# One exponential for four token tiles of A's keys, V's weights loaded early, and a new order

## The chip, the cores and the metric

The kernel runs on one core of a Trainium2 chip. A core has five engines with queues of their own: TensorE (PE) multiplies matrices, ScalarE (ACT) computes the exponentials, VectorE (DVE) evicts and combines, GpSimd (POOL) adds, SyncE (SP) issues transfers (ACT issues a few as well). PE's weight loads are listed as PEld. The time is the device time in microseconds (us), the median of several runs; lower is better.

## The reference

Two attention blocks on 2048 tokens of width 512, with 32 heads of 16 each, lie side by side in the output. A is linear attention: each key and query goes through phi, and the keys' products with V are summed over all tokens. B is full softmax attention.

```python
qkv = (x @ wqkv).reshape(B, S, 3, H, Dh).transpose(2, 0, 3, 1, 4)      # H = 32, Dh = 16, S = 2048
# A
phi = lambda t: jnp.where(t > 0, t + 1, jnp.exp(t)) + 1e-6
pq, pk = phi(q), phi(k)
kv = jnp.einsum("bhsd,bhse->bhde", pk, v)
z = jnp.einsum("bhsd->bhd", pk)
o = jnp.einsum("bhqd,bhde->bhqe", pq, kv) / (jnp.einsum("bhqd,bhd->bhq", pq, z)[..., None] + 1e-6)
# B
p = softmax(jnp.einsum("bhqd,bhkd->bhqk", q, k) * Dh ** -0.5)
o = jnp.einsum("bhqk,bhkd->bhqd", p, v)
# both: o.transpose(0, 2, 1, 3).reshape(B, S, D) @ wo;  out = concatenate([a, b], axis=-1)
```

## The kernel before

**B's scores.** They are cut into 2048 blocks of 128 keys by 512 queries for one head. Four heads share PE at a time, in groups g of 32 rows; a unit u is four heads (one of each row group) and one of four chunks of 512 queries, 64 blocks. `NU` is 32 units. Each block is computed by one matmul (`qk`, L872) and goes one of two ways.

- The first way is ACT's. Three blocks, then two (`ABL`), lie in one of two PSUM buffers `SCR` (pS in the profile); one ACT instruction (L1049) takes their exponential into `PT`, a ring of 3 rows with 2 slots each. One product with V (`pv_cand`, L1130) then adds a block into the PSUM tile pPV.
- The second way approximates the exponential in integers. DVE scales a block out of one of two PSUM banks `DBANK` (pD) into int16 (`d_emit`, L957), and those bits, read as float16, are the first of three terms. POOL adds two shifts to two such blocks at a time (`shifts`, L981) for the other two terms. Each term has V scaled by its own factor, so a block costs PE three products, not one.

A unit's sum ends with a transpose, a reciprocal and a multiplication (`unit_done`, L1185 to L1197).

**Jobs.** Everything else comes in jobs with stages on several engines, which use the banks of pD: projections of B's Q, K (`proj_job`, L595) and V (`v4_job`, L678; evicted by L683, and scaled twice by L687), a bound on B's scores (`gram_job`, `flag_job`), A's work, and the output projections (`omm_job`, L788). For A, `akv_job` takes two token tiles of 128 and one of four groups bq of 128 columns: 16 matmuls (L709), two evictions by DVE into `KNa` and `VNa`, then `phi_stages`: ACT's exponential into `EA` (L698), and on DVE max(t, 0) + 1e-6 (L700) and min(exp, 1) + that (L701). `akvsum_job` multiplies the 16 tiles of KNa and VNa into the state. The next bq's keys wait for it. A's queries go through `phi_stages` as well, 512 columns at a time. DVE's instructions with the key `PORT` and POOL's additions are ordered by semaphores so that they don't run at the same time.

**The order.** It is planned when the kernel is built, not on the chip. The planner keeps a clock for each engine (T), candidates with costs and due times, and picks the next instruction one by one; what it appends is what each engine runs, in that order, with semaphores between them. The numbers by which it chooses (`NAMES`) come from the table `POLICY`, one row for each 8 us of its own PE clock, 86 rows; `SEED` is that of a small random term. Costs such as 0.051 + n * 0.000833 us for an exponential over n columns stand in the code. Jobs wait in lists: `urgent`, `early` (the first projections of B, ten of them), `bjobs`, `urgent2`, `ajobs`. `d_pick` decides whether a block may go the second way now. `filler` puts matmuls that change nothing (zeros into pPV, L1348, or the identity into a free bank, L1357) into gaps of PE's plan that are long enough; `pe_opt` wraps each candidate of PE and adds `PH` where PE changes its kind of work.

**The loads.** SP issues B's x and weights in a fixed order, ACT two of them; V's columns of B's weights come as one load after the first transposing load of x.

**The end.** The last four token tiles' output projections are prepared by `pre_job`; `last_job` adds the last matmul (L815), an eviction (by ACT, ACT, DVE, ACT) and the store (L820), issued by SP after DVE's eviction and by ACT after its own.

Of the kernel before, what the change touches and what calls it, by code (L numbers as in the profile page):

```python
# [232 lines left out]
def bass_concat_heads__linear_attn_block__softmax_full_mha__prompt_kernel(nc, A_x, A_wqkv, A_wo, B_x, B_wqkv, B_wo, out):  # L233
# [14 lines left out]
    UB = NT * 4  # L248
    DEND = 12
# [4 lines left out]
    POLICY = [  # L254
        (0.15, 3.5, 4.2, 0, 3, 4, 32, 3.0, 1.0, 16, 10.0, 0.0, 0, 0, 0, 1, 0.0, 0.0, 2.0),
        (0.25, 3.5, 4.2, 0, 3, 4, 20, 3.0, 1.0, 16, 10.0, 0.0, 0, 0, 0, 1, 0.0, 0.0, 1.0),
        (0.25, 3.5, 3, 0, 3, 4, 20, 3.0, 0.5, 16, 10.0, 0.0, 0, 0, 0, 1, 0.0, 0.0, 1.0),
        (0.15, 3.5, 4.2, 0, 3, 4, 32, 3.0, 1.0, 16, 10.0, 0.0, 0, 0, 19, 1, 0.1, 0.0, 2.0),
        (0.15, 3.5, 4.2, 0, 3, 4, 32, 3.0, 1.0, 16, 10.0, 0.0, 0, 0, 19, 1, 0.1, 0.0, 2.0),
        (0.15, 3.5, 4.2, 0, 3, 4, 32, 3.0, 1.0, 16, 10.0, 0.0, 0, 0, 825, 1, 0.1, 0.0, 2.0),  # L260
        (0.15, 3.5, 4.2, 0.2, 3, 4, 32, 3.0, 1.0, 16, 10.0, 0.05, 0, 0, 298, 1, 0.1, 0.0, 2.0),
        (0.15, 3.5, 4.2, 0, 3, 4, 32, 3.0, 1.0, 16, 10.0, 0.0, 0, 0, 825, 1, 0.1, 0.0, 2.0),
        (0.15, 3.5, 4.2, 0, 3, 4, 32, 3.0, 1.0, 16, 10.0, 0.0, 0, 0, 825, 1, 0.1, 0.0, 2.0),
        (0.35, 3.5, 4.2, 0.3, 3, 4, 32, 3.0, 1.0, 16, 20.0, 0.0, 0, 0, 123, 1, 0.0, 0.0, 2.0),
        (0.15, 3.5, 4.2, 0, 3, 4, 32, 3.0, 1.0, 16, 10.0, 0.0, 3, 0, 726, 1, 0.0, 0.0, 2.0),
        (0.15, 3.5, 4.2, 0, 3, 8, 32, 3.0, 1.0, 16, 10.0, 0.0, 0, 0, 499, 1, 0.0, 0.0, 2.0),
        (0.15, 3.5, 4.2, 0, 3, 4, 32, 3.0, 1.0, 16, 10.0, 0.0, 3, 0.5, 8, 1, 0.0, 0.0, 0.3),
        (0.15, 3.5, 4.2, 0, 3, 7, 32, 3.0, 1.0, 16, 10.0, 0.0, 3, 0.5, 8, 1, 0.0, 0.0, 0.3),
        (0.15, 3.5, 4.2, 0, 3, 7, 32, 3.0, 1.0, 16, 10.0, 0.0, 3, 0.5, 155, 1, 0.0, 0.0, 0.3),
        (0.15, 3.5, 4.2, 0, 3, 4, 32, 3.0, 1.0, 16, 10.0, 0.0, 0, 0, 0, 1, 0.0, 0.0, 2.0),  # L270
        (0.15, 3.5, 4.2, 0, 3, 4, 32, 3.0, 1.0, 16, 10.0, 0.0, 0, 0, 7, 1, 0.0, 0.0, 2.0),
        (0.15, 3.5, 4.2, 0, 2, 4, 32, 3.0, 1.0, 16, 10.0, 0.0, 0, 0, 6, 1, 0.0, 0.0, 2.0),
        (0.15, 3.5, 4.2, 0, 3, 4, 32, 3.0, 1.0, 16, 10.0, 0.0, 0, 0, 7, 1, 0.0, 0.0, 2.0),
        (0.15, 3.5, 4.2, 0, 3, 4, 32, 3.0, 1.0, 16, 20.0, 0.0, 0, 0, 32, 1, 0.0, 0.0, 2.0),
        (0.15, 3.5, 4.2, 0, 3, 4, 32, 3.0, 1.0, 16, 10.0, 0.0, 0, 0, 0, 1, 0.0, 0.5, 2.0),
        (0.15, 3.5, 4.2, 0, 2, 4, 32, 3.0, 1.0, 16, 10.0, 0.0, 0, 0, 247, 1, 0.0, 0.0, 2.0),
        (0.15, 3.5, 2.6, 0, 3, 4, 32, 3.0, 1.0, 16, 20.0, 0.0, 0, 0, 633, 1, 0.2, 0.0, 2.0),
        (0.15, 3.5, 4.2, 0.1, 3, 4, 32, 3.0, 1.0, 16, 10.0, 0.0, 0, 0, 0, 1, 0.0, 0.0, 2.0),
        (0.15, 3.5, 2.6, 0, 3, 4, 32, 3.0, 1.0, 16, 20.0, 0.0, 0, 0, 633, 1, 0.2, 0.0, 2.0),
        (0.15, 3.5, 2.6, 0, 3, 4, 32, 3.0, 1.0, 16, 20.0, 0.0, 0, 0, 633, 1, 0.2, 0.0, 2.0),  # L280
        (0.15, 3.5, 2.6, 0, 3, 4, 32, 3.0, 1.0, 16, 20.0, 0.0, 0, 0, 229, 1, 0.2, 0.0, 2.0),
        (0.15, 3.5, 2.6, 0, 3, 4, 32, 3.0, 1.0, 16, 20.0, 0.0, 0, 0, 229, 1, 0.2, 0.0, 2.0),
        (0.15, 2.5, 4.2, 0, 3, 4, 32, 3.0, 1.0, 16, 10.0, 0.0, 0, 0, 0, 4, 0.0, 0.0, 2.0),
        (0.05, 3.5, 4.2, 0, 3, 4, 32, 3.0, 1.0, 16, 40.0, 0.0, 0, 0, 603, 1, 0.0, 0.0, 2.0),
        (0.05, 3.5, 4.2, 0, 3, 4, 32, 3.0, 1.0, 16, 40.0, 0.0, 0, 0, 603, 1, 0.0, 0.0, 2.0),
        (0.05, 3.5, 4.2, 0, 3, 4, 32, 3.0, 1.0, 16, 40.0, 0.0, 0, 0, 557, 1, 0.0, 0.0, 2.0),
        (0.35, 3.5, 3, 0, 3, 4, 32, 3.0, 1.0, 16, 40.0, 0.0, 0, 0, 910, 1, 0.0, 0.0, 2.0),
        (0.35, 3.5, 3, 0, 3, 4, 32, 3.0, 1.0, 16, 40.0, 0.0, 0, 0, 910, 1, 0.0, 0.0, 2.0),
        (0.15, 3.5, 3, 0, 3, 4, 32, 3.0, 1.0, 16, 10.0, 0.0, 0, 0, 0, 1, 0.0, 0.0, 2.0),
        (0.35, 3.5, 3, 0, 3, 4, 32, 3.0, 1.0, 16, 40.0, 0.0, 0, 0, 910, 1, 0.0, 0.0, 2.0),  # L290
        (0.15, 3.5, 3, 0, 3, 4, 32, 3.0, 1.0, 16, 10.0, 0.0, 0, 0, 0, 1, 0.0, 0.0, 0.3),
        (0.15, 3.5, 4.2, 0, 3, 4, 32, 3.0, 1.0, 16, 10.0, 0.0, 0, 0, 0, 1, 0.0, 0.0, 2.0),
        (0.15, 3.5, 4.2, 0, 3, 4, 32, 9.0, 1.0, 16, 10.0, 0.0, 0, 0, 0, 1, 0.0, 0.0, 2.0),
        (0.05, 3.5, 4.2, 0.2, 3, 4, 32, 3.0, 1.0, 16, 10.0, 0.0, 0, 0, 832, 1, 0.0, 0.0, 2.0),
        (0.15, 3.5, 3, 0, 3, 4, 32, 3.0, 1.0, 16, 10.0, 0.0, 0, 0, 0, 1, 0.0, 0.0, 2.0),
        (0.15, 3.5, 3, 0, 4, 4, 32, 3.0, 1.0, 16, 10.0, 0.0, 0, 0, 0, 1, 0.0, 0.0, 2.0),
        (0.15, 3.5, 3, 0, 4, 4, 32, 3.0, 1.0, 16, 10.0, 0.1, 0, 0, 390, 1, 0.0, 0.0, 2.0),
        (0.15, 3.5, 3, 0, 4, 4, 32, 3.0, 1.0, 16, 10.0, 0.1, 0, 0, 390, 1, 0.0, 0.0, 2.0),
        (0.15, 3.5, 4.2, 0, 3, 4, 32, 3.0, 1.0, 16, 10.0, 0.0, 0, 0, 0, 1, 0.0, 0.0, 2.0),
        (0.15, 3.5, 3, 0, 4, 4, 32, 3.0, 1.0, 16, 10.0, 0.1, 0, 0, 639, 4, 0.0, 0.0, 2.0),  # L300
        (0.15, 3.5, 3, 0, 4, 4, 32, 3.0, 1.0, 16, 10.0, 0.1, 0, 0, 438, 4, 0.0, 0.0, 2.0),
        (0.15, 3.5, 3, 0, 4, 4, 32, 6.0, 1.0, 16, 10.0, 0.1, 0, 0, 75, 4, 0.0, 0.0, 2.0),
        (0.15, 3.5, 3, 0, 4, 4, 32, 6.0, 1.0, 16, 10.0, 0.0, 0, 0, 456, 4, 0.0, 0.0, 0.3),
        (0.15, 3.5, 3, 0, 4, 4, 32, 6.0, 1.0, 16, 10.0, 0.1, 1.5, 0, 811, 4, 0.1, 0.0, 2.0),
        (0.15, 3.5, 3, 0, 4, 4, 32, 6.0, 1.0, 16, 10.0, 0.1, 1.5, 0, 697, 4, 0.1, 0.0, 2.0),
        (0.15, 3.5, 3, 0, 4, 4, 32, 6.0, 1.0, 16, 10.0, 0.1, 1.5, 0, 4, 4, 0.1, 0.0, 1.0),
        (0.15, 3.5, 3, 0, 4, 4, 20, 6.0, 1.0, 16, 10.0, 0.1, 1.5, 0, 697, 4, 0.1, 0.0, 2.0),
        (0.15, 3.5, 3, 0, 4, 4, 32, 6.0, 1.0, 16, 10.0, 0.1, 1.5, 0, 4, 4, 0.1, 0.0, 1.0),
        (0.15, 3.5, 3, 0, 4, 4, 20, 6.0, 1.0, 16, 10.0, 0.1, 1.5, 0, 697, 4, 0.1, 0.0, 2.0),
        (0.15, 3.5, 4.2, 0, 3, 4, 32, 3.0, 1.0, 16, 10.0, 0.0, 0, 0, 0, 4, 0.0, 0.0, 2.0),  # L310
        (0.15, 3.5, 3, 0, 4, 4, 20, 6.0, 1.0, 8, 10.0, 0.1, 1.5, 0, 697, 4, 0.1, 0.0, 2.0),
        (0.15, 3.5, 3, 0, 4, 4, 20, 6.0, 1.0, 8, 10.0, 0.1, 1.5, 0, 697, 4, 0.1, 0.0, 2.0),
        (0.15, 3.5, 3, 0, 4, 4, 20, 6.0, 1.0, 8, 10.0, 0.1, 1.5, 0, 697, 4, 0.1, 0.0, 2.0),
# [35 lines left out]
    with es:  # L349
# [1189 lines left out]
```

## Time and profile before

| what | value |
|---|---|
| median of 5 runs | 700.96 us (700.47 to 702.76) |
| the profiled execution | 701.14 us, its span 699.4 us |
| granted clock of PE, mean | 0.998 |
| exponentials of B's scores on ACT (L1049) | 583 |
| scalings on DVE (L957), of 512 and of 1024 columns | 576 and 7 |
| additions on POOL (L981) | 295 |
| exponentials of A's keys (256 columns) and queries (512) on ACT | 32 and 16 |

The span runs from the first to the last instruction of the program. A line of groups gives the line of the kernel, the engine, the operation, what it writes and reads with partitions x elements, the number of such instructions, their busy time together, the mean ns of one, and the idle time of the engine just before them with what ended most of it. Instructions of one engine can overlap, so mean times number can be more than the busy time. A line of the timeline gives the start, the length of a run of like instructions, and in brackets the idle time before. A line of waits gives who waited for whom: us in total, times, the longest. A line of windows gives a stretch, its length, the busy time and number of the instructions named, PE's granted clock, and the share and rate of the DMA engines.

### The profile page before, as it was taken

The numbers are of one execution on the slowest core, as the hardware profiler recorded it, in microseconds if no ns is written. First come the engines' busy times: TensorE is split into PE (matmuls) and PEld (weight loads), VectorE is DVE, ScalarE is ACT, GpSimd is POOL, SyncE is SP. The second block draws the span as 40 slices with busy tenths as digits, with TensorE's granted clock in tenths as the row PEclk, the third lists the DMA queues.
The fourth block names the chain that finished last, engine by engine and source line by source line (L and its number), as shares of the span: only waits on it lengthen the run. The fifth ranks groups of instructions, "written<-read, shape, count | busy, mean of one in ns | idle before, by whom it ended". The sixth has DMA issues, their size and how long they took to land.

```text
span 699.4 us, 15831 instructions
## 1 busy us (share of the span) xinstructions
PE 666.8 (95%) x6735; PEld 226.7 (32%) x6735; DVE 566.9 (81%) x1017; ACT 682.7 (98%) x639; POOL 575.0 (82%) x347
## 2 busy tenths in 40 slices
PE   8999999999999999999999999999999999999996
PEld 5323443333333434332222233322222222222221
DVE  5788888888888888878888888878888888877872
ACT  5999999999999999999999999999999999999995
POOL 6498568778888878877999879999879987998992
PEclk9999999999999999999999999999999999999999
DMA  9900000000000000010100000000001000011001
GB/s 219 233 1 3 2 1 7 11 10 8 2 2 1 2 1 2 3 43 10 26 23 16 9 1 16 25 17 16 16 19 29 23 5 29 23 31 31 17 19 40
DMA packets 35788, 17.34 MB, mean 25 GB/s; under 512 B 26496, under 2 KB 35200, under 8 KB 35712
## 3 DMA queue, kind: packets, MB, share of 16 engines
q1 hardware_dynamic: 34480, 15.48, 9.0%
q8 instruction: 55, 0.90, 0.5%
q10 hardware_dynamic: 1232, 0.79, 0.4%
q14 instruction: 21, 0.17, 0.1%
HBM read 4.72 MB, written 4.19 MB: 13 GB/s over the span
## 4 chain that ended last, share of the span: by engine, by line
ACT 87%; PE 9%; DVE 2%; POOL 1%; issue 0%; ACTq 0%; POOLq 0%
ACT PT L1049 85%; PE pPV L1130 3%; ACT EA L698 2%; PE pS L872 2%; DVE DI L957 1%; PE pD L872 1%; POOL DI L981 1%; PE pD L678 1%; PE pD L595 1%; PE pD L709 1%; PE pD L1207 0%; PE pD L788 0%; PE pS L570 0%; ACT KNa L563 0%; DVE KNa L701 0%
## 5 line engine op out<-in xcount | busy, mean ns | idle before, releaser
L1049 ACT ACTIVATE PT<-pS 128x1536 f16<-128x1536 f32 x583 | 669.4, 1339 | 3.8 <-PE pS L872 1.8
L981 POOL TENSOR_TENSOR DI<-DI,SHC 128x1024 int32<-128x1024 int32 x295 | 550.5, 1892 | 100.9 <-DVE DI L957 33.7
L957 DVE TENSOR_SCALAR DI<-pD 128x512 int16<-128x512 f32 x583 | 387.8, 690 | 68.5 <-PE pD L872 58.1
L1130 PE MATMUL pPV<-DI,VV 128*17 128x512 f16 x1770 | 256.8, 381 | 1.2 <-DVE OT L1185 0.9
L1130 PE MATMUL pPV<-PT,VV 128*17 128x512 f16 x1458 | 251.0, 382 | 1.3 <-ACT PT L1049 1.2
L872 PE MATMUL pS<-QT,KM 32*128 32x512 bf16 x1458 | 227.0, 384 | 14.3 <-ACT PT L1049 9.0
L872 PE MATMUL pD<-QT,KM 32*128 32x512 bf16 x590 | 211.4, 384 | 3.7 <-DVE DI L957 2.6
L872 PEld LDWEIGHTS pS<-QT,KM 32*128 32x128 bf16 x1458 | 55.7, 90 | 194.4 <-ACT PT L1049 144.6
L1130 PEld LDWEIGHTS pPV<-DI,VV 128*17 128x17 bf16 x1770 | 55.4, 88 | 69.1 <-issue 49.5
L1130 PEld LDWEIGHTS pPV<-PT,VV 128*17 128x17 bf16 x1458 | 54.9, 88 | 60.3 <-issue 43.3
L872 PEld LDWEIGHTS pD<-QT,KM 32*128 32x128 bf16 x590 | 51.4, 91 | 62.4 <-DVE DI L957 39.0
L709 PE MATMUL pD<-Wa,xTa 128*128 128x128 bf16 x512 | 36.6, 220 | 0.4 <-DVE DI L957 0.4
L595 PE MATMUL pD<-xTb,Wb 128*128 128x512 bf16 x120 | 32.3, 382 | 1.0 <-DVE DI L957 0.6
L709 PEld LDWEIGHTS pD<-Wa,xTa 128*128 128x128 bf16 x512 | 28.8, 98 | 12.3 <-DVE DI L957 6.1
L1192 POOL TENSOR_TENSOR OT<-OT,ZR 128x256 bf16<-128x256 f32 x31 | 19.2, 620 | 9.6 <-DVE KNa L701 8.2
L1185 DVE STREAM_TRANSPOSE OT<-pPV 128x512 f32<-128x512 f32 x31 | 22.0, 709 | 0.8 <-PE pPV L1130 0.6
L678 PE MATMUL pD<-Wb,xTb 128*128 128x128 bf16 x256 | 17.8, 220 | 0.8 <-DVE DI L957 0.7
L788 PE MATMUL pD<-WOa,ONT 128*128 128x512 bf16 x64 | 18.3, 383 | 0.2 <-DVE DI L957 0.2
L736 PE MATMUL pD<-xTa,Wa 128*128 128x512 bf16 x64 | 17.6, 383 | 0.1
L712 DVE CAST KNa<-pD 128x256 bf16<-128x256 f32 x32 | 13.4, 419 | 4.0 <-PE pD L709 4.0
L678 PEld LDWEIGHTS pD<-Wb,xTb 128*128 128x128 bf16 x256 | 14.3, 98 | 6.5 <-DVE DI L957 3.0
L604 DVE CAST QT<-pD 128x512 bf16<-128x512 f32 x15 | 10.3, 687 | 7.4 <-PE pD L595 7.4
(106 smaller groups left out, 307.8 us busy)
## 6 DMA issues: line engine op xcount, KB each, us to landing
out_dram<-OB SPq DMA_DIRECT2D x16, 128.0 KB, 1.9
out_dram<-KNa SPq DMA_DIRECT2D x13, 128.0 KB, 1.7
Wa<-in_A_wqkv_dram SPq DMA_DIRECT2D x1, 1536.0 KB, 7.2
KM<-KR SPq DMA_DIRECT2D x96, 16.0 KB, 1.8
Wb<-in_B_wqkv_dram SPq DMA_DIRECT2D x2, 384.0 KB, 4.4
Wb<-in_B_wqkv_dram SPq DMA_DIRECT2D x1, 512.0 KB, 4.5
WOa<-in_A_wo_dram SPq DMA_DIRECT2D x1, 512.0 KB, 8.0
VNa<-in_B_wo_dram SPq DMA_DIRECT2D x1, 512.0 KB, 4.0
```

The costliest lines, as they stand in the source:

```text
L595: return e.matmul(f32v(bk), lhsT=Wb[:, cc, kind * 512 + Gp * 128:kind * 512 + Gp * 128 + 128], rhs=xTb[:, cc, sc * 512:(sc + 1) * 512], st ...
L678: return e.matmul(f32v(bk)[:, tl * 128:(tl + 1) * 128], lhsT=xTb[:, cc, t * 128:(t + 1) * 128], rhs=Wb[:, cc, 1024 + Gp * 128:1024 + Gp * ...
L709: return e.matmul(f32v(bk)[:, 128 * x:128 * x + 128], lhsT=xTa[:, cc, (t + i_) * 128:(t + i_ + 1) * 128], rhs=Wa[:, cc, c0:c0 + 128], star ...
L736: return e.matmul(f32v(bk), lhsT=Wa[:, cc, bq * 128:(bq + 1) * 128], rhs=xTa[:, cc, sc * 512:(sc + 1) * 512], start=(cc == 0), stop=(cc == 3))
L788: return e.matmul(f32v(bk), lhsT=src, rhs=WO[:, hb, :], start=(hb == 0), stop=(hb == 3))
L872: return e.matmul(dst, lhsT=KM[32 * g:32 * g + 32, Gp % 2, e_, j * 128:(j + 1) * 128], rhs=QT[32 * g:32 * g + 32, Gp % 2, c * 512:(c + 1) ...
L957: sch.add("dve", lambda e: e.tensor_scalar(DI[:, buf, 0, i * 512:(i + n) * 512], DB[:, bi * 512:(bi + n) * 512], ESC, EB, op0=ALU.mult, op ...
L981: sch.add("pool", lambda e: e.tensor_tensor(DI32[:, buf, 1:3, 0:w], DI32[:, buf, 0, 0:w].unsqueeze(1).broadcast_to([128, 2, w]), SHC32[:]. ...
L1049: sch.add("act", lambda e: e.activation(PT[:, row, c0:c0 + w], SCR[sl][:, 0:w], ACTF.Exp, scale=SC), reads=skeys(sl), writes=[("PT", row, ...
L1130: sch.add("pe", lambda e, g=g, vk=vk, c0=c0, P=P, first=first, last_=last_: e.matmul(PVb[32 * g:32 * g + 17, 0:512], lhsT=VV[:, Gp % 2, vk ...
L1185: sch.add("dve", lambda e: e.transpose(OT[:, 0, :], PVb[:, 0:512]), reads=[("PV", g) for g in range(4)], writes=[("OT", 0)])
L1192: (ml, 0.65, f_op(ml, lambda e: e.tensor_tensor(xn[:, :, 16 * e_:16 * e_ + 16], o[:, :, 0:16], zr.unsqueeze(2).broadcast_to([128, 16, 16]) ...
```

## The change

- `akv_job`: the first of two pairs of token tiles ends with its evictions and gives `ak0`. The second pair takes exponential, maximum and sum for all four tiles at once (512 columns). `akvsum_job` waits for these.
- V's columns of the first four heads' group (128 of 512) are loaded by a load of their own, third on ACT's queue; the remaining 384 stay where the whole load was. `v4_job` waits for the part it needs.
- The early jobs begin with V's first four tiles, and `d_pick` lets no block go the second way while more than `EN` = 5 early jobs are left.
- The store of the last job's tiles 0 and 1 is issued by SP, only that of tile 3 by ACT.
- `filler` also counts `PH` where the filler would be followed by PE work of the kind that ran before it, and it places one even where it doesn't fit when the planned PE work in the last 3.41 us is below 60% (`HWIN`, `HMIN`, `streamed`); the next PE work is then planned later. `thin` makes the denominators' matmuls (8 columns) count little in that measure.
- All 86 rows of `POLICY` are replaced (some values recur at other places).

```diff
+    EN = 5
     POLICY = [
...
+        load(Wb[:, :, 1024:1152], wbv[:, :, 1024:1152], [("Wb", 2, 0)], queue="act")
...
             if t0 == 4:
-                load(Wb[:, :, 1024:1536], wbv[:, :, 1024:1536], [("Wb", 2)])
+                load(Wb[:, :, 1152:1536], wbv[:, :, 1152:1536], [("Wb", 2, 1)])
...
+        HWIN, HMIN = 3.41, 0.6
+        thin = [False]
...
-            st = halves(mm, [("Wb", 2)] + [("xTb", t) for t in ts], n=16, parts=2, dur=0.0555)
+            st = halves(mm, [("Wb", 2, min(Gp, 1))] + [("xTb", t) for t in ts], n=16, parts=2, dur=0.0555)
...
-            st += phi_stages(256, KNa[:, t:t + 2, :].rearrange("p t n -> p (t n)"), [("KNa", t), ("KNa", t + 1)])
-            return Job(st, [("xTa", t), ("xTa", t + 1)] + ([("akv", bq - 1)] if bq else []),
+            if (t // 2) % 2 == 0:
+                return Job(st, [("xTa", t), ("xTa", t + 1)] + ([("akv", bq - 1)] if bq else []), [(3, ("ak0", bq, t))], rel=3, **kw)
+            st += phi_stages(512, KNa[:, t - 2:t + 2, :].rearrange("p t n -> p (t n)"), [("KNa", t + x) for x in range(-2, 2)])
+            return Job(st, [("xTa", t), ("xTa", t + 1), ("ak0", bq, t - 2)],
                        [(5, ("ak", bq, t))], rel=3, **kw)
...
-            return Job(st, [("ak", bq, t) for t in range(0, NT, 2)], [(3, ("akv", bq)), (5, ("rha", bq))], **kw)
+            return Job(st, [("ak", bq, t) for t in range(2, NT, 4)], [(3, ("akv", bq)), (5, ("rha", bq))], **kw)
...
-                                      reads=obk(o2), queue="sp" if lane == "dve" else "act", force_signal=True))
+                                      reads=obk(o2), queue="act" if tl == 3 else "sp", force_signal=True))
...
-            if bi is None or jfree[bi] > at or not d_open() or d_backlog(at) > P["DBL"]:
+            if len(early) > EN or bi is None or jfree[bi] > at or not d_open() or d_backlog(at) > P["DBL"]:
...
-        early += [proj_job(0, 1, 1, fast=True), v4_job(0, 0), proj_job(0, 2, 1, fast=True), v4_job(1, 0), proj_job(0, 3, 1, fast=True),
-                  v4_job(2, 0), v4_job(3, 0)]
+        ek, ev_ = (lambda c_: proj_job(0, c_, 1, fast=True)), (lambda t4: v4_job(t4, 0))
+        early += [ev_(0), ek(1), ek(2), ev_(1), ek(3), ev_(2), ev_(3)]
...
+        def streamed(end):
+            u, k_ = 0.0, len(streams) - 1
+            while k_ >= 0 and streams[k_][1] > end - HWIN:
+                u += min(streams[k_][1], end) - max(streams[k_][0], end - HWIN)
+                k_ -= 1
+            return u
+
+        def filler(gap, nmode):
             t_ = T["pe"]
+            forced = t_ > 15.0 and left[NU - 1] > 8 and streamed(t_ + gap) < HMIN * HWIN
...
-                    if cost + FMARG > gap:
-                        return
+                    if cost + FMARG + (PH if pmode[0] == nmode != "v" else 0.0) > gap and not forced:
+                        return t_
+                    nforced[0] += cost + FMARG > gap
+                    forced = False
...
             if eng == "pe":
-                filler(st - T["pe"])
+                st = max(st, filler(st - T["pe"], run_.mode))
```

## The prediction

> **What bounds the kernel now.** I read the page first, then the groups by shape, then the timeline of ScalarE (ACT), the waits of GpSimd (POOL), and the start and the end instruction by instruction.
>
> ```profile
> PE 666.8 (95%) x6735; PEld 226.7 (32%) x6735; DVE 566.9 (81%) x1017; ACT 682.7 (98%) x639; POOL 575.0 (82%) x347
> ACT 87%; PE 9%; DVE 2%; POOL 1%; issue 0%; ACTq 0%; POOLq 0%
> ```
>
> The first line is the page's busy time, the second its chain that ended last. ACT is the bound: 98% busy, 87% of the chain. PE at 95% is close behind it.
>
> ```profile
> L1049 ACT ACTIVATE PT<-pS 128x1536 f16<-128x1536 f32 x292 | 453.4, 1553 | 3.6 <-PE pS L872 1.8 <-PE pD L872 1.3 <-issue 0.4
> L1049 ACT ACTIVATE PT<-pS 128x1024 f16<-128x1024 f32 x291 | 327.5, 1125 | 0.3 <-PE pD L872 0.2
> L701 DVE SCALAR_TENSOR_TENSOR KNa<-EA,KNa 128x256 bf16<-128x256 bf16 x32 | 13.6, 425 | 1.1
> L701 DVE SCALAR_TENSOR_TENSOR PQT<-EA,PQT 128x512 bf16<-128x512 bf16 x16 | 11.1, 692 | 0.6
> L700 DVE TENSOR_SCALAR KNa<-KNa 128x256 bf16<-128x256 bf16 x32 | 6.9, 217 | 1.7 <-POOL DI L981 1.3
> L700 DVE TENSOR_SCALAR PQT<-PQT 128x512 bf16<-128x512 bf16 x16 | 4.5, 283 | 0.8 <-POOL DI L981 0.7
> ```
>
> These are groups by shape (busy us, mean ns of one, idle before). ACT hardly waits between the exponentials of B: 3.9 us in all. Their durations overlap, so the price of a block (128 keys by 512 queries) is the page's union, 669.4 us over 292x3 + 291x2 = 1458 blocks: 0.459 us. The other 2048 - 1458 = 590 blocks go the second way: DVE (L957), one POOL addition for two blocks (L981), and three products instead of one on PE. From ACT's first exponential (9.34) to its last (690) that is 680.7/590 = 1.154 us a block.
>
> So the end is 9.34 us of start, ACT's work, and 9.3 us of tail. A block that goes the second way frees 0.459 us on ACT; if everything ends earlier by x, the second way also loses x/1.154 blocks. Hence x = 0.715 times what is freed, since 1/(1 + 0.459/1.154) = 0.715.
>
> **A's keys: one exponential, maximum and sum for four tiles.** Sixteen of each take the place of 32. ACT's timeline prices the exponential:
>
> ```profile
> 70.18 0.63 ACT L698 ACTIVATE EA<-KNa 128x256 bf16<-128x256 bf16 x1
> 70.48 8.45 ACT L1049 ACTIVATE PT<-pS 128x1536 f16<-128x1536 f32 x7
> ...
> 304.85 0.68 ACT L698 ACTIVATE EA<-PQT 128x512 bf16<-128x512 bf16 x1
> 305.37 6.94 ACT L1049 ACTIVATE PT<-pS 128x1536 f16<-128x1536 f32 x6
> ```
>
> What counts is the step to the next start: 0.30 us for 256 elements, 0.52 for 512 (A's queries have that shape). Saved: 16 x (2 x 0.30 - 0.52) = **1.3 us of ACT**. DVE by the rows above: 16 x (2 x (0.217 + 0.425) - (0.283 + 0.692)) = 16 x 0.309 = 4.9 us. Beyond that, POOL's additions and these pairs exclude each other by semaphores (the key PORT):
>
> ```profile
> POOL DI L981 <- DVE KNa L701: 24.1, 20, 2.0
> ...
> POOL OT L1192 <- DVE KNa L701: 8.2, 7, 2.4
> ```
>
> In the stretch from 70 to 295 us POOL waits 32.3 us, 27 times, for the sums of keys. Half as many episodes, each longer by 0.33 us, could save 16 us of it. What becomes of the freed time isn't shown. Low end: nothing, since PE is 96% busy there (216.3 of 224.5) and each more block costs it three products. By DVE: 4.9/1.154 = 4 blocks. By POOL: 16/1.154 = 14 blocks, the high end. I take the middle of the two ends, **7 blocks, 3.2 us of ACT**, as in that stage both are partly idle (DVE 189.2 of 224.5 busy, POOL 175.9) and each waits for the other.
>
> What is held longer: behind the pair on DVE stand the evictions L957, 0.33 us later, 16 times; PE's next score matmul waits for them. Today all such waits are 39.0 us in 109, and ACT has its other PSUM buffer of scores to work on meanwhile, so nothing; uncovered it would be 5 us. The first two tiles' keys wait for the second two's eviction; only the state sum (L722) wants them, four times, and PE has scores to do meanwhile. Nothing.
>
> **Early V weights, V first, and no second-way block until five early jobs are left.** The start now (timeline):
>
> ```profile
> 9.34 6.88 ACT L1049 ACTIVATE PT<-pS 128x1536 f16<-128x1536 f32 x6 [0.97 <-PE pD L872]
> 15.39 0.69 DVE L683 CAST VV<-pD 128x512 bf16<-128x512 f32 x1 [0.93 <-PE pD L678]
> 16.69 0.39 PE L1130 MATMUL pPV<-PT,VV 128*17 128x512 f16 x3
> 17.89 2.37 ACT L1049 ACTIVATE PT<-pS 128x1536 f16<-128x1536 f32 x2 [1.67 <-PE pS L872]
> 20.59 39.97 ACT L1049 ACTIVATE PT<-pS 128x1536 f16<-128x1536 f32 x35 [0.34 <-PE pD L872]
> ```
>
> Six exponentials fill all six buffers of PT; no product can free one until the first V is evicted (16.1). ACT stands 1.67 us, later 0.34. With V's columns loaded early, V is projected at 9 to 10 us and the buffers come free in time: **2.0 us of ACT**. Ends: 2.0, and 0 if the first K block is late instead: V's DVE work (0.69 + 0.64) is put before K's eviction, which ended near 14.4, so it moves to 15.8; the 16 first blocks last ACT until 9.34 + 16 x 0.459 = 16.7 as long as the second way takes none of them. The gate sees to that, and this is its price: 4 evictions of that way (L957) lie between 9.34 and 20.59. Ends: all 4 lost, or none (the projections' DVE work moves forward and leaves room later). I take 2: **-0.9 us of ACT**.
>
> The load itself is 128 KB issued third on ACT's queue: 0.49 us by its neighbours, ahead of the table load. ACT then idles 2.42 us before its first copy, which hides it; without that cover, 0.49. On SP's queue the V load shrinks from 512 to 384 KB in its place. The DMA engines are full then (191 GB/s up to 9.34 us), so 128 KB moved forward can delay what starts the kernel by 0.7 us; I take 0, as it's issued behind all that, and keep 0.7.
>
> [...]
>
> **The tail.** Two of the last stores move from ACT's queue to SP's.
>
> ```profile
> 694.45 0.36 ACTq L820 DMA_DIRECT2D out_dram<-KNa  x1
> 694.91 0.60 ACT L563 ACTIVATE KNa<-pS 128x512 bf16<-128x512 f32 x1 [0.49 <-ACT KNa L563]
> ```
>
> The last copy stands behind two issues (0.38 and 0.36). Without them it starts when its matmul is done (693.67 + 0.60, some 694.3): **0.6 us**, undivided, since nothing else runs. SP's queue stood empty for 13.5 us by then, so the two stores (0.33 us of issue each) pass before the third copy's. Next late is that store, issued at 694.81 already. Low end 0.1.
>
> **Fillers and orders.** 25 fillers (L1348, L1357) run now, some 0.33 us apart. The new rule makes fewer fit, but forces one where a planned window of 3.41 us is under 60% streamed. Taken at 0: PE stands 144.6 us, 335 times, before scores that wait for ACT. Without that cover 25 forced ones cost 8 us. All 86 rows of the order's table change; no row prices that. Its ends come from the stages:
>
> ```profile
> 70.00:294.50 224.50, 170.03 (x91) 1.00 0.02 4
> 304.00:587.00 283.00, 237.57 (x128) 1.00 0.07 18
> ```
>
> These are the POOL additions alone, in A's key and query stage: 2.47 and 2.21 us each. At the faster pace the key stage would hold 101.6, so 21 blocks more; at the slower one the query stage 114.6, so 27 fewer. In time -6.9 to +8.9 us. I take 0, the pace as it is.
>
> **Sum.** (1.3 + 3.2 + 2.0 - 0.9) x 0.715 + 0.6 = 4.6 us. The profiled execution took 701.14 (span 699.4 and 1.7 around it), 0.18 above the median: 696.5 there, 696.4 as a median, forecast **696.5**; its own range 694.5 to 698.4.
>
> **Rivals.** (1) *The freed time isn't used*: no more second-way blocks, and the gate costs all four. (1.3 + 0 + 2.0 - 1.8) x 0.715 + 0.6 = 1.7, so 699.3, spread 698.4 to 701.5. For it: PE at 95%. Against: POOL's 32.3 us. (2) *The key stage reaches the query stage's pace*: 14 blocks beyond my 7, 14 x 0.459 x 0.715 = 4.6 more, 691.9. For it: POOL busy in 13.86 of 25 us between 75 and 100, the emptiest stretch. Against: the projections and evictions of A's keys stay as many as they are. (3) *Slower, by PE's clock*: an order that leaves PE thin in the key stage loses the clock. In the last 9.4 us the granted clock is 0.87 with PE busy 2.66; elsewhere 1.00. The 28 warm-up matmuls of 128 columns took 3.17 us (0.113 each), sixteen like ones of A's keys in the chain 1.03 (0.064), so a slow stretch loses 43% of its time: 1.5 us in a window of 3.41. Three windows eat the gain, four make it slower than before by 1.4 us; at five it is 696.5 + 7.5 = 704.0. Against: the clock never dropped mid-run, and the forced fillers guard it.
>
> **How the numbers follow.** Forecast 0.46, (1) 0.22, (2) 0.18, (3) 0.14. What 0.2% is (1.4 us, about what a measurement of this kernel can tell from no change) cuts at 699.6 and 702.4: faster 0.46 + 0.18 + half of (1) = 0.75, same 0.10, slower 0.14 and a rest of (1), 0.15. The range runs from 691.5, just under (2), to 701.5, the top of (1); (3) and a third of (2) lie outside.
>
> **What would show it.** 16 key exponentials of 512, no ACT gap of over 1 us near 16 us, first product before 13 us; some 597 blocks through L957; POOL's waits for key sums near 17 us; no 0.49 idle before the last copy; clock 1.00 up to 690. I am wrong if blocks through L957 fall under 585, or if the first exponential comes after 10 us.

## The result, and the profile after

| | before | after |
|---|---|---|
| median | 701.55 us (56 runs, 700.21 to 703.21) | 699.52 us (31 runs, 698.22 to 702.32) |
| ratio after/before | | 0.9976 [0.997, 0.9981] |
| profiled execution, span | 701.14, 699.4 us | 700.15, 698.4 us |
| first exponential of B's scores | 9.34 us | 8.62 us |
| from there to the tail's first copy by ACT | 683.38 us | 683.93 us |
| from that copy to the end of the span | 6.68 us | 5.85 us |
| blocks the second way | 590 | 591 |

The change makes the kernel 0.24% faster, 1.7 us by the ratio, 2.0 by the medians. PE's mean granted clock varies from one execution to the next in both: 0.993 to 0.999 (median 0.996) in the 59 executions of before that stood beside the experiments, 0.994 to 1.000 (median 0.999) in 33 of after. Where it is 0.998 or more, the medians are 700.9 us (16 executions) and 699.2 us (21), again 1.7 us apart. In the profiled executions the long middle part, which ACT bounds, didn't become shorter: the 1.0 us between the spans comes from an earlier first exponential and a shorter tail.

First the page of the kernel after: the busy line and the chain.

```profile
PE 665.5 (95%) x6758; PEld 222.8 (32%) x6758; DVE 563.5 (81%) x992; ACT 681.0 (98%) x623; POOL 575.9 (82%) x348
ACT 82%; PE 11%; DVE 3%; DMA 1%; SPq 1%; POOL 1%; issue 0%; DVEq 0%; POOLq 0%
```

ACT is still the bound, with 1.7 us less work: 16 x 0.08 = 1.3 us for the keys and 0.46 for one block more that goes the second way. New in the chain are a DMA and SP's queue (SPq), 1% each: a transfer now stands on the path. The groups by shape of the kernel after (busy us, mean ns of one, idle before):

```profile
L1057 ACT ACTIVATE PT<-pS 128x1536 f16<-128x1536 f32 x291 | 452.4, 1555 | 3.7 <-PE pS L880 2.0 <-PE pD L880 1.6
L1057 ACT ACTIVATE PT<-pS 128x1024 f16<-128x1024 f32 x292 | 329.5, 1129 | 1.9 <-PE pS L880 1.7 <-issue 0.2
...
L702 ACT ACTIVATE EA<-KNa 128x512 bf16<-128x512 bf16 x16 | 11.5, 717 | 0.0
...
L705 DVE SCALAR_TENSOR_TENSOR KNa<-EA,KNa 128x512 bf16<-128x512 bf16 x16 | 11.1, 692 | 0.6
...
L704 DVE TENSOR_SCALAR KNa<-KNa 128x512 bf16<-128x512 bf16 x16 | 4.5, 283 | 0.7 <-POOL DI L989 0.6
```

The keys' sixteen exponentials, sums and maxima have the durations of the queries' rows. But the idle time before B's exponentials rose from 3.9 to 5.6 us. ACT's timeline shows where (start, length, what, idle before):

```profile
8.62 5.97 ACT L1057 ACTIVATE PT<-pS 128x1536 f16<-128x1536 f32 x5 [0.97 <-PE pS L880]
16.04 1.02 ACT L1057 ACTIVATE PT<-pS 128x1024 f16<-128x1024 f32 x1 [1.45 <-PE pS L880]
18.08 60.56 ACT L1057 ACTIVATE PT<-pS 128x1536 f16<-128x1536 f32 x53 [1.03 <-PE pS L880]
...
88.27 4.63 ACT L1057 ACTIVATE PT<-pS 128x1536 f16<-128x1536 f32 x4 [0.83 <-PE pD L880]
```

The stalls of 1.67 and 0.34 us are gone, and 1.45 and 1.03 have come in their place. Five smaller ones follow the 0.83 up to 160 us; the six add up to 2.05 us, against 0.70 for the three gaps of before after 21 us. None of the six stands behind a pair of maximum and sum on DVE; before the 0.83, PE projects A's keys and V one after the other (85.18 to 87.15), and the scores come after that. PE's timeline of the kernel after, at the same place:

```profile
11.54 0.40 PE L1138 MATMUL pPV<-PT,VV 128*17 128x512 f16 x4
...
12.38 0.39 PE L880 MATMUL pS<-QT,KM 32*128 32x512 bf16 x3 [0.24 <-ACT PT L1057]
14.19 1.27 PE L599 MATMUL pD<-xTb,Wb 128*128 128x512 bf16 x4 [1.42 <-DMA xTb<-in_B_x_dram]
15.39 0.60 PE L880 MATMUL pS<-QT,KM 32*128 32x512 bf16 x2
```

V came in time: the first product starts at 11.54 us, not 16.69. What is late now is B's x. PE runs its list in order; the projection of the second K block wants tokens that the second transposing load of x brings, and PE stands 1.42 us at it, with the score matmuls that ACT waits for behind it. SP's queue in the same stretch, first of before, then of after:

```profile
1.81 3.92 SPq L431 DMA_TRANSPOSE xTb<-in_B_x_dram  x1
5.79 0.57 SPq L418 DMA_DIRECT2D Wb<-in_B_wqkv_dram  x1
```
```profile
1.82 4.45 SPq L433 DMA_TRANSPOSE xTb<-in_B_x_dram  x1
6.32 0.57 SPq L419 DMA_DIRECT2D Wb<-in_B_wqkv_dram  x1
6.94 6.58 SPq L433 DMA_TRANSPOSE xTb<-in_B_x_dram  x2
```

The issue of a transposing load holds the queue for 2.95 to 4.45 us in after, and the load of V's other 384 columns still stands ahead of the second one. In before a V load, of all 512 columns, stood there too. The second transposing load alone, in before and in after (duration of its issue in ns, its start, and the us from its start to the landing of its data):

```profile
L431 SPq DMA_TRANSPOSE xTb<-in_B_x_dram x1: 3592/3592/3592, 6.4 to 6.4; - x1
...
DMA to landing us min/median/max: 6.0/6.0/6.0
```
```profile
L433 SPq DMA_TRANSPOSE xTb<-in_B_x_dram x1: 3594/3594/3594, 6.9 to 6.9; - x1
...
DMA to landing us min/median/max: 7.2/7.2/7.2
```

So the tokens land at 12.4 us in before and at 14.1 in after, while PE asks for them at 12.77 in after (14.19 less 1.42). The change moved both: PE's demand forward and the tokens back. The first transposing load's issue already takes 4.45 us instead of 3.92, and the only transfer ahead of it that is new is the early load of V's first 128 columns on ACT's queue (e7 below leaves it out).

Now stretches of the kernel after (start:end, length, busy us and number for PE, PEld, DVE, ACT, POOL, then PE's granted clock, the DMA share and GB/s):

```profile
13.00:15.00 2.00, 0.81 (x4) 0.31 (x4) 0.00 (x0) 1.59 (x2) 0.00 (x0) 0.97 0.87 173
15.00:17.00 2.00, 2.00 (x16) 0.97 (x14) 1.41 (x2) 0.96 (x1) 0.00 (x0) 0.50 1.01 262
17.00:19.00 2.00, 2.00 (x17) 0.80 (x13) 0.24 (x1) 0.97 (x2) 0.00 (x0) 0.68 1.15 264
19.00:20.59 1.59, 1.59 (x17) 0.42 (x16) 1.52 (x4) 1.59 (x3) 0.00 (x0) 1.00 1.01 228
```

After the wait PE's granted clock is 0.50 from 15 to 17 us. Counted as time at a clock of 0.50, the first three stretches hold 0.12 + 2.0 + 1.28 = 3.4 us of slow clock (each is 2.00 us long, times what it lacks to 1.00, divided by 0.50). The second stall, 1.03 us, falls into it; where the same order kept its clock (e2 below), it was 0.18.

The second way in the start and in A's key stage (the scalings L965 alone) and POOL's waits in that stage (70 to 295 us):

```profile
9.34:20.59 11.25, 0.00 (x0) 0.85 1.11 225
...
70.00:294.50 224.50, 124.15 (x188) 1.00 0.02 4
```
```profile
POOL DI L989 <- DVE DI L965: 18.9, 18, 4.3
POOL DI L989 <- DVE KNa L705: 16.7, 10, 2.6
...
POOL OT L1200 <- DVE KNa L705: 1.4, 1, 1.4
```

The start has no block of the second way (before 4), the key stage has 188 (before 182). POOL's waits for key sums fell from 32.3 to 18.1 us, while its waits for blocks to be scaled rose there from 9.3 to 18.9. Last, the tail of the kernel after:

```profile
692.55 1.08 ACT L567 ACTIVATE KNa<-pD 128x512 bf16<-128x512 f32 x2 [2.88 <-PE pD L823]
...
694.14 0.60 ACT L567 ACTIVATE KNa<-pS 128x512 bf16<-128x512 f32 x1 [0.50 <-PE pS L823]
694.77 0.37 ACTq L828 DMA_DIRECT2D out_dram<-KNa  x1
```

The two copies now follow each other without a store between them, and the last one waits for its matmul, no longer for ACT's queue.

### The profile page after: what moved, and what is told of

The parts are those of the page before. It is cut to its first block, busy times and chain, and to the rows that moved or that the text cites. A ratio compares the mean times of both kernels' runs of the same rounds, so it can differ in the third digit from the quotient of the medians.

```text
span 698.4 us, 15827 instructions
## 1 busy us (share of the span) xinstructions
PE 665.5 (95%) x6758; PEld 222.8 (32%) x6758; DVE 563.5 (81%) x992; ACT 681.0 (98%) x623; POOL 575.9 (82%) x348
## 4 chain that ended last, share of the span: by engine, by line
ACT 82%; PE 11%; DVE 3%; DMA 1%; SPq 1%; POOL 1%; issue 0%; DVEq 0%; POOLq 0%
ACT PT L1057 80%; PE pPV L1138 3%; PE pS L880 3%; ACT EA L702 2%; DVE DI L965 1%; DMA xTb<-in_B_x_dram 1%; PE pD L682 1%; PE pD L599 1%; POOL DI L989 1%; PE pD L713 1%; PE pD L880 1%; SPq L433 1%; PE pD L642 1%; PE pD L796 1%; DVE VV L691 0%
## 5 line engine op out<-in xcount | busy, mean ns | idle before, releaser
L965 DVE TENSOR_SCALAR DI<-pD 128x512 int16<-128x512 f32 x590 | 389.2, 684 | 73.9 <-PE pD L880 64.9
L1138 PE MATMUL pPV<-DI,VV 128*17 128x512 f16 x1773 | 245.6, 382 | 1.2 <-DVE OT L1193 0.9
L1138 PEld LDWEIGHTS pPV<-DI,VV 128*17 128x17 bf16 x1773 | 51.6, 88 | 64.1 <-issue 46.8
L1138 PEld LDWEIGHTS pPV<-PT,VV 128*17 128x17 bf16 x1457 | 51.7, 88 | 62.5 <-issue 48.9
L713 PEld LDWEIGHTS pD<-Wa,xTa 128*128 128x128 bf16 x512 | 28.8, 98 | 14.4 <-issue 6.7
L687 DVE CAST VV<-pD 128x512 bf16<-128x512 f32 x16 | 11.0, 689 | 6.0 <-PE pD L682 5.9
```

What stands on the lines that cost most here:

```text
L713: return e.matmul(f32v(bk)[:, 128 * x:128 * x + 128], lhsT=xTa[:, cc, (t + i_) * 128:(t + i_ + 1) * 128], rhs=Wa[:, cc, c0:c0 + 128], star ...
L965: sch.add("dve", lambda e: e.tensor_scalar(DI[:, buf, 0, i * 512:(i + n) * 512], DB[:, bi * 512:(bi + n) * 512], ESC, EB, op0=ALU.mult, op ...
L1138: sch.add("pe", lambda e, g=g, vk=vk, c0=c0, P=P, first=first, last_=last_: e.matmul(PVb[32 * g:32 * g + 17, 0:512], lhsT=VV[:, Gp % 2, vk ...
```

## The experiments

All ratios are to the kernel before. Except in e8, what an experiment cuts or leaves out doesn't change the order of anything else.

**e1, the rest of V's weights behind the transposing loads.**

```diff
             if t0 == 4:
-                load(Wb[:, :, 1152:1536], wbv[:, :, 1152:1536], [("Wb", 2, 1)])
+                pass
...
-        load(Wb[:, :, 640:1024], wbv[:, :, 640:1024], [("Wb", 1, g) for g in range(1, NGP)])
+        load(Wb[:, :, 640:1024], wbv[:, :, 640:1024], [("Wb", 1, g) for g in range(1, NGP)]); load(Wb[:, :, 1152:1536], wbv[:, :, 1152:1536], [("Wb", 2, 1)])
```

> The changed kernel with one edit: the rest of V's weights (384 KB) is loaded behind all transposing loads of B's x and the other weights, where SP issued it between the first and the second. Every engine's order stays the same. Theory A (the start gave back what the keys won): x tiles 8 to 11 land some 1.2 us earlier, PE no longer stands 1.4 us at 12.8, ACT's two gaps there (1.45 and 1.03 us) shrink to under 1.2 together, the clock between 9.34 and 20.59 reads 1.00 and not 0.85, and the time falls by 1.0 to 2.5 us against the changed kernel: ratio to before 0.994 to 0.9962. Rival B (the new order itself is worth no more, the start doesn't matter): ratio 0.9970 to 0.9981 as the changed kernel.

Measured: 697.86 us, 0.9946 [0.9933, 0.9958]. ACT's timeline, PE's and SP's:

```profile
9.20 67.15 ACT L1057 ACTIVATE PT<-pS 128x1536 f16<-128x1536 f32 x59 [0.97 <-PE pS L880]
```
```profile
13.29 1.04 PE L599 MATMUL pD<-xTb,Wb 128*128 128x512 bf16 x4
```
```profile
1.82 9.58 SPq L433 DMA_TRANSPOSE xTb<-in_B_x_dram  x3
11.44 1.68 SPq L419 DMA_DIRECT2D Wb<-in_B_wqkv_dram  x3
```
```profile
L433 SPq DMA_TRANSPOSE xTb<-in_B_x_dram x1: 2900/2900/2900, 6.5 to 6.5; - x1
...
DMA to landing us min/median/max: 5.1/5.1/5.1
```

The transposing loads are issued by 11.4 us instead of 13.5, the second one's tokens land at 11.6 instead of 14.1 (more than the 1.2 us that were expected), the projection doesn't wait, and ACT runs 59 exponentials without a gap. The clock is 1.00 up to the tail. Whether the place in the queue or the 384 KB on the DMA engines made the difference, the run doesn't tell apart. One load in another place is worth 0.0030 of the time, 2.1 us. The wait for x is the cause of what was missing at the start; this version is faster than both kernels. In the stretch from 9.34 to 20.59 us it has two blocks of the second way.

**e2, the last stores back on ACT's queue.**

```diff
-                                      reads=obk(o2), queue="act" if tl == 3 else "sp", force_signal=True))
+                                      reads=obk(o2), queue="sp" if lane == "dve" else "act", force_signal=True))
```

> The changed kernel with the last stores issued by ACT again, as before. Everything else is the same. Theory: the tail is longer by 0.6 us (the last copy starts 0.4 to 0.6 later), ratio to before about 0.9985. Rival (SP's store ends as late as ACT's, so it's nothing): ratio 0.9976, the span from ACT's last exponential of B to the end the same within 0.1.

Measured: 699.06 us, 0.9972 [0.996, 0.9983]; against the change itself the time can't tell it apart. Its profile can. The tail in ACT's timeline:

```profile
691.13 0.60 ACT L567 ACTIVATE KNa<-pD 128x512 bf16<-128x512 f32 x1 [2.88 <-PE pD L823]
691.76 0.37 ACTq L828 DMA_DIRECT2D out_dram<-KNa  x1
692.23 0.60 ACT L567 ACTIVATE KNa<-pD 128x512 bf16<-128x512 f32 x1 [0.51 <-ACT KNa L567]
...
693.32 0.60 ACT L567 ACTIVATE KNa<-pS 128x512 bf16<-128x512 f32 x1 [0.49 <-ACT KNa L567]
```

From the first tail copy to the end of the span it is 6.4 us here, 5.85 after: some 0.5 us in the tail. It is hidden in the time because the start went better in this profile, which says something of its own (PE's timeline):

```profile
14.19 1.04 PE L599 MATMUL pD<-xTb,Wb 128*128 128x512 bf16 x4 [1.21 <-DMA xTb<-in_B_x_dram]
```

The order is that of the change, but PE waits 1.21 us, not 1.42; the clock stays at 1.00, and ACT's stalls are 0.79 and 0.18 us. So the change's start comes in two forms, from one execution to the next.

**e3, the keys of four tiles in two halves, in the change's order.** Exponential, maximum and sum are cut (`cut=2` in the keys' call of `phi_stages`).

```diff
+            ectr[0] += 1; vs = [slice(x * w, (x + 1) * w) for x in range(cut)]
...
+                ("act", 0.051 + n * 0.000833, both(*[f_op("act", lambda e, v_=v_: e.activation(EA[:, q, v_], t_ap[:, v_], ACTF.Exp), list(keys), [("EA", q, x)]) for x, v_ in enumerate(vs)])),
...
+            st += phi_stages(512, KNa[:, t - 2:t + 2, :].rearrange("p t n -> p (t n)"), [("KNa", t + x) for x in range(-2, 2)], cut=2)
```

> The changed kernel, in its own order, with each of the 16 key quads computed as two halves of 256 columns again (two exponentials, and maximum and sum twice), one right after the other. Theory A: this adds 16 x 0.08 = 1.3 us on ACT and 4.9 us on DVE; the first counts in full, of the second a part, since the order can't move blocks: 1.3 to 3.5 us slower than the changed kernel, ratio to before 0.9995 to 1.0026. Rival (the keys' instructions are hidden, the merge is worth nothing): ratio 0.9970 to 0.9981.

Measured: 702.39 us, 1.0017 [1.0008, 1.0026], 0.0041 above the change: 2.9 us. Without the larger pieces all the gain is gone. In its profile the start has the good form (PE waits 1.29 us, the clock stays at 1.00, ACT idles 1.05 us); from the first exponential to the first tail copy it takes 685.88 us, 3.6 more than e2 with the same form of the start (682.31).

**e4, no fillers** (PE's 46 matmuls that change nothing are left out).

```diff
-                    sch.add("pe", lambda e, g=g: e.matmul(PVb[32 * g:32 * g + 32, 0:512], lhsT=ZW[:],
+                    (lambda *a_, **k_: None)("pe", lambda e, g=g: e.matmul(PVb[32 * g:32 * g + 32, 0:512], lhsT=ZW[:],
```

> The changed kernel in its own order without any of the matmuls that only fill gaps. Theory (they stand where PE waits for ACT): ratio as the changed kernel, 0.9970 to 0.9981, clock as there. Rival 1 (forced ones delay scores): 1 to 3 us faster, 0.9935 to 0.996. Rival 2 (they keep the clock up): granted clock under 0.99 in the middle of the run, slower than before.

Measured: 700.19 us (698.92 to 704.41), 0.9998 [0.9981, 1.0015]. Its mean granted clock goes from 0.987 to 0.999 between executions, the five longest times (702.38 and more) with the five lowest clocks (0.991 and less). In its profile (0.997) the only loss is at the start: PE waits 1.47 us for x, the clock falls to 0.59 and 0.56 from 15 to 19 us, and ACT idles 1.28, 1.02 and 0.22 us. Where the executions with a lower clock lose it, no profile shows.

**e5, e1 without fillers, and e6, e1 without the seven forced ones.** e5 has the edit of e4, e6 leaves a filler out where it doesn't fit its gap:

```diff
+                    (sch.add if cost + FMARG <= gap else (lambda *a_, **k_: None))("pe", lambda e, g=g: e.matmul(PVb[32 * g:32 * g + 32, 0:512], lhsT=ZW[:],
```

> The run with V's rest late (0.9946), in its own order, without any of the 46 matmuls that only fill gaps. Its start has no gap, so what the fillers do is seen alone. Theory F (they keep the clock up where PE is thin): granted clock 0.990 to 0.996 in place of 0.998 to 1.000, single runs spread by several us, 1 to 3 us slower: ratio to before 0.996 to 0.999. Rival (they cost and bring nothing; the slower median of the first run without them came from its start): ratio 0.9935 to 0.9955, clock as it was.

> The run with V's rest late without the 7 fillers that the new rule forces into gaps too short for them; the other 39 stay. Theory F1 (the forced ones stand where the clock would fall): half or more of what all fillers do, clock under 0.998, ratio 0.995 to 0.998. Rival F2 (the 39 that fit do it): ratio 0.9935 to 0.9955, clock 0.998 to 1.000.

Measured: e5 697.49 us, 0.9948 [0.9935, 0.9961], clock 0.997 to 1.0; e6 698.03 us, 0.9951 [0.9938, 0.9964]. Both are equal to e1. Where PE didn't stand at the start, the fillers brought nothing and cost nothing in these two runs. So the loss in e4 goes together with the gap at the start; how, isn't shown.

**e7, V's weights as one load at the old place, no early load.**

```diff
-        load(Wb[:, :, 1024:1152], wbv[:, :, 1024:1152], [("Wb", 2, 0)], queue="act")
+        pass
...
-                load(Wb[:, :, 1152:1536], wbv[:, :, 1152:1536], [("Wb", 2, 1)])
+                load(Wb[:, :, 1024:1536], wbv[:, :, 1024:1536], [("Wb", 2, 0), ("Wb", 2, 1)])
```

> The changed kernel in its own order with V's weights as one load at the old place on SP, so without the early load. Theory: the load lands at 10.3 to 10.8 us; V's matmuls stand second in PE's order at 8.5 and hold up everything behind them, ACT's second exponential starts 1.5 to 2 us late, and a part of that comes back because the next x tiles are the limit anyway: 0.5 to 1.5 us slower than the changed kernel, ratio to before 0.9983 to 0.9997. Rival (the early load costs the start what it brings): ratio 0.9960 to 0.9976.

Measured: 699.08 us, 0.9977 [0.9962, 0.9992], the change's own time; the loss that was expected didn't come. ACT's and PE's timelines:

```profile
11.99 65.80 ACT L1057 ACTIVATE PT<-pS 128x1024 f16<-128x1024 f32 x58 [1.73 <-PE pS L880]
```
```profile
10.56 1.07 PE L682 MATMUL pD<-Wb,xTb 128*128 128x128 bf16 x16 [1.79 <-DMA Wb<-in_B_wqkv_dram]
```

Now PE waits 1.79 us for V's weights, and when it reaches the second K block (14.73) the x tiles are there. SP's queue and the second transposing load:

```profile
1.82 3.85 SPq L433 DMA_TRANSPOSE xTb<-in_B_x_dram  x1
```
```profile
L433 SPq DMA_TRANSPOSE xTb<-in_B_x_dram x1: 3925/3925/3925, 6.3 to 6.3; - x1
...
DMA to landing us min/median/max: 6.5/6.5/6.5
```

Its tokens land at 12.8 us, 1.3 earlier than in after, though 512 columns of V stand ahead of them and not 384. So the early load itself made x late: with it the issue of the first transposing load took 4.4 to 4.7 us (after, e1 to e4), without it 3.85 and 3.92 (e7 and before); with it and the rest of V between the x loads the tokens landed at 14.1 to 14.4 (after, e2, e3, e4), without it at 12.8 and 12.4. Either V or x makes PE wait; the early load alone passes the wait on to the next transfer. In these runs it is worth something only with the rest of V behind x (e1).

**e8, e1 with the 86 rows of the table before.**

```diff
     POLICY = [
-        (0.15, 3.5, 4.2, 0, 4, 4, 32, 3.0, 1.0, 16, 10.0, 0.0, 0, 0, 0, 1, 0.0, 0.0, 2.0),
...
+        (0.15, 3.5, 4.2, 0, 3, 4, 32, 3.0, 1.0, 16, 10.0, 0.0, 0, 0, 0, 1, 0.0, 0.0, 2.0),
+        (0.25, 3.5, 4.2, 0, 3, 4, 20, 3.0, 1.0, 16, 10.0, 0.0, 0, 0, 0, 1, 0.0, 0.0, 1.0),
...
```

> The run with V's rest late, but the 86 rows of the order's table from the kernel before: all edits, and an order that was not searched with them. Theory (the table fits one set of edits only, and most of what an order is worth lies in it): 15 to 40 us slower than before, ratio 1.02 to 1.06, with ACT idle for 20 us and more and some 588 blocks by the second way. Rival (the edits bring their gain under any table): ratio 0.992 to 1.000.

Measured: 730.18 us, 1.0411 [1.039, 1.0431]. ACT's waits:

```profile
ACT PT L1057 <- PE pD L880: 19.8, 20, 3.7
```

The table of before doesn't fit the changed jobs, so this run can't say what the new order is worth by itself.

**e9 and e10, one half of e3 each, on e1.** e9 cuts the keys' exponentials alone into halves, e10 their maxima and sums alone (edits as in e3, in one of the two stages).

> The run with V's rest late (0.9946), in its own order, with the exponential alone of each of the 16 key quads in two halves of 256 columns; maximum and sum stay whole. Theory (ACT's part counts in full): 16 x (0.62 - 0.52) = 1.6 us slower, from the steps that the run with both in halves showed: ratio to before 0.9966 to 0.9972. Rival (what the halves cost, 2.9 us, came from DVE): ratio 0.9940 to 0.9955.

> The run with V's rest late (0.9946), in its own order, with maximum and sum alone of each of the 16 key quads in two halves; the exponential stays whole. Theory (in a fixed order DVE's 4.9 us more are mostly hidden, but push some scores): 0.5 to 1.5 us slower, ratio to before 0.9951 to 0.9968, POOL's wait for key sums up by 3 us. Rivals: all of it counts (3 us and more, ratio over 0.999), or nothing (0.9940 to 0.9949).

Measured: e9 698.76 us, 0.9963 [0.9951, 0.9976], 0.0017 over e1, 1.2 us, about as much as the intervals allow by chance; e10 700.75 us, 0.9993 [0.9983, 1.0004], 0.0047 over e1, 3.3 us. From the first exponential to the tail's first copy it is 682.19 and 684.06 us against 681.10 in e1: +1.1 and +3.0. Two exponentials of 256 in a row took a step of 0.62 us against 0.52 for one of 512, 1.6 us in sixteen; by the profiles 1.1 of it counts. e10 adds 4.9 us of DVE work by the rows above (16 x 0.309), and 3.0 of it ends in the time, more than was expected. POOL's waits for key sums in e10:

```profile
POOL DI L989 <- DVE KNa L705: 19.3, 10, 2.9
...
POOL OT L1200 <- DVE KNa L705: 1.8, 1, 1.8
```

They are only 1.7 us longer than in e1 (18.0 and 1.4). The rest goes other ways: ACT's waits for scores behind a pD bank rose from 1.6 to 2.7 us. How the 3.0 us is made up is not settled.

The start in profiles with the change's order (keys undivided, so that the last column can be compared; e5 and e6 have e1's start):

| | PE waits for a load | lowest clock, 13 to 19 us | ACT idle at the start | first exponential to first tail copy |
|---|---|---|---|---|
| e1 | none | 1.00 | 0 | 681.10 |
| e2 | 1.21 (x) | 1.00 | 0.97 | 682.31 |
| e7 | 1.79 (V) | 1.00 | 1.73 | 682.89 |
| after | 1.42 (x) | 0.50 | 2.48 | 683.93 |
| e4 | 1.47 (x) | 0.56 | 2.52 | 683.96 |

In these five profiles each us in which ACT idles at the start cost 1.0 to 1.25 us: in the fixed order nothing made up for it.

## Why the prediction was wrong

The time was 2.0 us shorter by the medians, 1.7 by the ratio, where 4.6 was forecast. The direction, and faster by over 0.2%, came true, by little; the measured time is in the wide range and outside the forecast's own, and it lies at the time of rival (1), for another reason: with all four blocks lost and none gained, that rival leaves 590 - 4 - 1.7/1.154, some 585 blocks, and there are 591.

**The step that failed** is the start: "V is projected at 9 to 10 us and the buffers come free in time: 2.0 us of ACT". Its first half came true (first product at 11.54, asked for before 13). But ACT's idle time there became 2.48 us, or 0.97 where the clock held, not 0. The text looked for what is late next among the evictions of K (the first K block at 15.8; it was evicted by 12.74) and not among the loads. K's second block now asks for x at 12.77, and its tokens land at 14.1, 1.7 us later than in before. e1 takes that wait away and gains 2.1 us, which brings the gain to 3.8 and the time, 697.86, into the forecast's own range. That one wait is most of the miss.

**Inside it, a term put at nothing:** "128 KB moved forward can delay what starts the kernel by 0.7 us; I take 0, as it's issued behind all that". The first exponential wasn't delayed: it came at 8.58 to 9.26 us in the profiles with the early load, at 8.81 without it (e7), at 9.34 in before. But the x loads behind it were: the first transposing load's issue by 0.5 to 0.8 us, and the second one's tokens by 1.3 (from e7 to after). In before the two loads with rows of 256 B landed 4.2 and 4.5 us after their issue, the 512 KB one with rows of 1,024 B after 4.5; no run tells whether the length of the rows or just the 128 KB delayed x. And e7 shows that without e1's move the early load, credited with the 2.0 us, brings nothing.

**The gate.** Two blocks lost were taken as the middle of none and four. From 9.34 to 20.59 us none is left in after, but that is the wait once more: in e1, with the same order, two lie in that stretch, and after and e1 both have 591 in all. What the gate costs by itself wasn't tried, since without it everything after the start has to be planned anew.

**A's keys: the size fits, the way is only in part shown.** 4.5 us of ACT's time were forecast, 3.2 us in the end (4.5 x 0.715). Cutting both pieces costs 2.9 us by the medians (e3), and singly 1.1 to 1.2 and 3.0 to 3.3. ACT's part is as forecast. For the rest the forecast was that waits of POOL turn into 7 more blocks of the second way. The waits fell, to 18.1 us where some 17 were named (11 of 1.65 us on average in place of 27 of 1.20). The 16 us of the high end had a slip, though: with each wait 0.33 us longer, as the text itself says, half as many would save 32.3 - 13.5 x 1.53 = 11.7 us, 10 blocks, and the middle would be 5. And the scalings in the key stage went from 182 to 188, but from 304 to 587 us, where no keys are, they went from 253 to 260 as well, so the count doesn't show that the keys' merge brought the six. e10 shows what the larger maxima and sums are worth in an order that was planned for them, where no block can move. That the size came out near 3 us is in part luck. The evictions behind the longer pair, taken at nothing, were not seen to cost anything.

**Blocks of the second way.** "Some 597" was a slip of the prediction against its own sum: 590 + 7 - 2 for the gate - 4.6/1.154 for the earlier end is 591, which was also measured. It doesn't judge the forecast.

**The tail, right.** 0.6 us forecast, some 0.5 by e2.

**Fillers, right** at 0 where the start has no gap (e5, e6).

**The order, too cheap at 0.** Between 88 and 160 us ACT's gaps are 2.05 us, and e1 has the same ones (0.83, 0.28, 0.17, 0.27, 0.15 and 0.34). Before had 0.70 after the start; by the factor 0.715 the 1.35 more are 1.0 us. That is argued from the profile, not tried: e8 shows why the table can't be undone by itself.

**Rival (3), the clock,** came in a small way and at another place. "Clock 1.00 up to 690" is wrong: 0.50 after 15 us in the profile. From e2 (clock 1.00) to after (0.50) the middle part grows by 683.93 - 682.31 = 1.6 us, 0.2 of it by the longer wait for x, close to the 1.5 us that the prediction gave for one slow stretch. That was an estimate, 43% of the planner's 3.41 us: the 28 matmuls it comes from ran at a granted clock of 1.00 (before, 1.59 to 4.71 us), and measured in after are some 3.4 us at 0.50. "The clock never dropped mid-run" rested on one execution of before: of 59 executions, 33 had a mean clock of 0.996 or less and took 701.8 us in the median. Where they lose it, no profile shows. Of the executions of the kernel after, those with a mean clock of 0.998 or more took 698.2 to 700.0 us, those of 0.997 or less 700.1 to 702.3.

In all: 4.6, less 2.1 for the wait for x, less 1.0 for the later gaps, is 1.5; measured is 1.7 to 2.0. Of these terms only the first is shown, and it is the larger. The two profiles agree with it: ACT's work fell by 1.7 us, but its idle time rose by 0.47 at the start (2.01 to 2.48), by 1.35 in the later gaps and by 0.25 before the first tail copy (2.63 to 2.88), and so the part between grew by some 0.5 us and didn't shrink by 4.0.

## What to carry to other kernels

When a load is moved forward so that a stall goes, follow every instruction that now comes sooner back to its own load, and look at which queue that load stands in and behind what, and also at what the moved load does to transfers on other queues: 128 KB on ACT's queue made tokens on SP's 1.3 us late. In this fixed order the wait passed to the next transfer (1.79 us for V in e7, 1.42 for x in after), and early V weights were worth nothing until the rest of V went behind x. Small pairs on an engine that the kernel's semaphores let shut out another one can be worth merging even where that engine isn't the bound: DVE is 81% busy, and cutting the sixteen pairs in two cost 3.0 to 3.3 us (e10). And read the profile of a run beside its median: here the profiled execution had the bad form of the start, and to judge by the mean clock (0.998 or more in 21 of 33) most of the others hadn't.

## What the runs showed of the hardware

After waits of 1.42 (after) and 1.47 us (e4) PE's granted clock fell: to 0.50 from 15 to 17 us and 0.68 from 17 to 19 in after, to 0.59 and 0.56 in the same stretches of e4. Counted as time at 0.50 that is some 3.4 us in each. After waits of 1.21 (e2), 1.29 (e3) and 1.79 us (e7) it stayed at 1.00 up to 20.59 us. So the length of the wait alone didn't decide; what did, no trace here shows.

In these runs a load on one queue went with slower transfers on another: with 128 KB more on ACT's queue, the first transposing load on SP's took 4.4 to 4.7 us to issue (after, e1 to e4), without it 3.85 and 3.92 us (e7, before). Its data landed 6.6 us after its start in after, 5.9 in before.

The start of one and the same order varies by more than some of the terms in the sum: the first sixteen PE transposes took 1.07 us in the profile of after and 1.89 in e1 (and in before), and the first exponential of the same order came between 8.58 and 9.26 us.
